# Starting every SBUF tile on a multiple of 128 bytes in a retention + GLU + SwiGLU kernel

## The chip, the cores and the metric

The kernel runs on one core of one Trainium2 chip. The metric is the time of one execution on the device in microseconds. Before the change three runs took 669.10, 670.97 and 668.92 us, median 669.1 us.

## The reference

Three stages follow one another. Retention: per batch and head a state is decayed by gamma and grows by the outer product of key and value; the output is the query times the state. Then a feed-forward layer, `(a * b) @ w_out`, on 1536 tokens of width 512 with hidden width 1536. Then RMS normalisation with a gain, and a second layer with a SiLU gate.

```python
for t in range(S):                       # S = 768, 2 batches, 8 heads, head_dim 64
    state = gamma * state + k[t] outer v[t]
    y[t] = q[t] @ state / sqrt(64)
x = y.reshape(1536, 512)
x = ((x @ w_a) * (x @ w_b)) @ w_out                       # first layer, d_ff 1536
xn = x / sqrt(mean(x * x) + 1e-6) * rms_g
out = (silu(xn @ w_gate) * (xn @ w_val)) @ w_out2         # second layer
```

## The kernel before

**Numbers.** Every operand of the two layers is held as a pair of fp32r tiles, `hi` and `lo`, whose sum is the value, and each product is made of three matmuls: hi*hi, hi*lo and lo*hi. `x_tiles` allocates the pairs of activations (`xh`, `xl`, in the second layer `nh`, `nl`), `conv_w` makes the pairs of weights (`wh`, `wl`), and `second` in `up` makes the pairs of hidden values (`hh`, `hl`).

**Units.** The work of the layers is cut into 72 units, in the order of layer, weight group `g` (4), token block `j` (3 blocks of 512 tokens) and hidden block `f` (3 of a group). A unit issues two runs of 12 matmuls in `up_half` (lines 170 to 172: four blocks of the width, three matmuls each), each with 512 columns, and later, in `down`, another 12 (lines 214 to 216 in the first layer, 218 to 220 in the second). So a unit has 36 matmuls of 512 columns and all units 72 x 36 = 2592. The `down` of a unit comes two or three units after its `up` (`LAG2`, `LAG`). In the up runs and the first layer's downs the weights are the stationary operand and the activations move; in the second layer's downs the hidden values are stationary and the weights move.

**Two sets of weight tiles.** A weight block `c` goes to `wps[c % RING]`, with `RING` 6: blocks 0 to 2 of each six, which are the groups with even `g`, go to the pool `wp`, which is made at the start; blocks 3 to 5, the groups with odd `g`, go to the pool `wq`, which is made after the retention (line 466). Half of the units, 36, work on `wp` tiles, and the other half on `wq` tiles. In time the groups alternate: even, odd, even, odd in either layer.

**Where the tiles lie.** The tiles of a pool lie end to end in a partition, in the order of first allocation, each begun on a multiple of 32 bytes; a pool that is closed (the retention's `ac`, `ap`, `a2`) gives its space to the pools made after it (`yp`, `wq`). The first tile, `rg_sb`, has 4 numbers (16 bytes) in each partition, and takes 32. `dk_sb` has 192 bytes and `gq_sb` 96. All other tiles that matter here have multiples of 512 bytes, but for the five small tiles of the normalisation (`me`, `t`, `r`, `rh`, `rl`, 16 bytes each, in `yp` ahead of `wq`). The program's list of allocations gives these byte addresses in the partition:

| tiles | first address | remainder by 128 | by 512 |
|---|---|---|---|
| `rg_sb` | 16512 | 0 | 128 |
| `ones`, `ones32`, `ident` | 16544 | 32 | 160 |
| `xh`, `xl`, `nh`, `nl` (pool `xp`) | 18080 | 32 | 160 |
| `wh`, `wl` in `wp` | 67232 | 32 | 160 |
| `hh`, `hl` and the other hidden tiles | 104096 | 32 | 160 |
| `raw`, `u`, `v`, `z` (pool `cp`) | 124576 | 32 | 160 |
| `dq_sb`, later `acc` of block 1 | 159392 | 32 | 160 |
| `dk_sb`, `gq_sb` | 161952, 162144 | 32, 96 | 160, 352 |
| `q`, `k`, `qd`, `vd`, `p`, `sd` of the retention | 162752 | 64 | 448 |
| `sq`, `d` | 175776 | 32 | 160 |
| `me`, `t`, `r`, `rh`, `rl` | 188064 | 32, 64, 96, 0, 32 | |
| `wh`, `wl` in `wq` | 188224 | 64 | 320 |

**Engines beside TensorE.** `conv_w` turns a loaded raw weight block (64-bit numbers) into a pair: two passes on ScalarE (lines 120, 121), five on VectorE (123 to 125, 134, 138), one on GpSimd (126), one more on ScalarE (136). 72 blocks are converted. `norm` squares a block's sums, adds them up by matmuls with `ones32` (264), computes the reciprocal root with a refinement step on tiles of 4 numbers (267 to 275), spreads it by a diagonal (278, GpSimd) and a matmul (284), and scales (290 to 294). The DMAs of the loads are issued by SyncE, those of the constants at the start by ScalarE. The order on each engine is that of the program text (`manual_schedule`).

Of the kernel before, what the change touches and what calls it, by code (L numbers as in the profile page):

```python
# [7 lines left out]
F32 = mybir.dt.float32  # L8
# [7 lines left out]
B, H, S, D = 2, 8, 768, 64  # L16
P = 128
# [5 lines left out]
CPB = S // C  # L23
NP = H // 2
KD = DM // P
NF = DFF // P
TB = 512
NB = NT // TB
CPT = TB // C
TPB = TB // P  # L30
# [9 lines left out]
BEGIN = {0: (1, 1), 1: (1, 1), 2: (0, 1)}  # L40
BEGIN |= {i: (i in (10, 13, 16, 19, 22), 1) for i in (*range(3, 34), *range(39, 66))}
LAG = 3
SIGN = -(1 << 31)

PARTS = KD, TPB
# [3 lines left out]
def retention_glu_swiglu(ctx: ExitStack, tc: tile.TileContext, qk, kv, dq, tri, dk, gq, eye, w1, w2, rg, out):  # L49
# [19 lines left out]
    cst = ctx.enter_context(tc.tile_pool(name="cst", bufs=1))  # L69
# [5 lines left out]

    y0 = ctx.enter_context(tc.tile_pool(name="y0", bufs=1))

    rg_sb = cst.tile([P, KD], F32, name="rg_sb")
    ones = cst.tile([P, P], F32R, name="ones")
    ones32 = cst.tile([P, P], F32, name="ones32")  # L80
    ident = cst.tile([P, 1, P], F32, name="ident")

    xs = {}

    def x_tiles(j, what):
        hi = xp.tile([P, KD, TB], F32R, tag="xh", name=f"{what}h{j}")
        lo = xp.tile([P, KD, TB], F32R, tag="xl", name=f"{what}l{j}")
        xs[what, j] = (hi, lo)
# [18 lines left out]
    def conv_w(i):  # L107
# [15 lines left out]
        nc.vector.tensor_scalar(ui, ui, 3, 0x7FFFFFFF, op0=ALU.logical_shift_left, op1=ALU.bitwise_and)  # L123
        nc.vector.scalar_tensor_tensor(ui, upper, SIGN, ui, op0=ALU.bitwise_and, op1=ALU.bitwise_or)
        nc.vector.tensor_scalar(zi, ui, -(1 << 23), None, op0=ALU.bitwise_and)  # L125
# [24 lines left out]
    def step(todo=beside):  # L150
        for g in list(todo):
            if next(g, g) is g:
                todo.remove(g)
# [21 lines left out]
    def up(i):  # L175
# [13 lines left out]
        def second():  # L189
            b = up_half(i, 1)  # L190
            h = hp.tile([P, TB], F32, tag="h", name=f"h{i}")
            hh = hp.tile([P, TB], F32R, tag="hh", bufs=LAG, name=f"hh{i}")
            hl = hp.tile([P, TB], F32R, tag="hl", bufs=LAG, name=f"hl{i}")
            nc.vector.tensor_tensor(h, b, gate[0], op=ALU.mult)  # L194
# [27 lines left out]
    def collect(i):  # L222
        ffn, g, j, f = units[i]
        if f % GRP < GRP - 1:
            return
        if g == 0:
            acc[ffn, j] = (yp if j else y0).tile([P, *((TPB, DM) if ffn else (KD, TB))], F32, tag=f"acc{j}", name=f"acc{ffn}_{j}")
        for m in range(PARTS[ffn]):
            collect_part(ffn, g, j, m)
        if ffn == 0 and g == NG - 1:  # L230
            norming.append(norm(j))
# [17 lines left out]
    def norm(j):  # L249
        y = acc[0, j]  # L250
        sq = yp.tile([P, KD, TB], F32, tag="sq", name=f"sq{j}")
        d = yp.tile([P, 2, TB], F32R, tag="d", name=f"d{j}")
        me, t, r, rh, rl = (yp.tile([P, TPB], F32, tag=w, name=f"{w}{j}") for w in ("me", "t", "r", "rh", "rl"))
        nc.scalar.activation(sq[:, 0:2, :], y[:, 0:2, :], AF.Square)
        nc.scalar.activation(sq[:, 2:4, :], y[:, 2:4, :], AF.Square)
        yield
        yield
        nc.vector.tensor_tensor(sq[:, 0:2, :], sq[:, 0:2, :], sq[:, 2:4, :], op=ALU.add)
        nc.vector.tensor_tensor(sq[:, 0, :], sq[:, 0, :], sq[:, 1, :], op=ALU.add)
        for _ in range(4):  # L260
            yield
        ms = sp.tile([P, TB], F32, tag="S", name=f"ms{j}")
        for c in range(TPB):
            nc.tensor.matmul(ms[:, c:c + 1], sq[:, 0, c * P:(c + 1) * P], ones32[:, 0:1], start=True, stop=True)
        yield

        nc.vector.tensor_scalar(me, ms[:, 0:TPB], 1.0 / DM, 1e-6, op0=ALU.mult, op1=ALU.add)
        nc.scalar.activation(t, me, AF.Sqrt)
        yield
        nc.vector.reciprocal(r, t)  # L270
        nc.vector.tensor_tensor(t, r, r, op=ALU.mult)
        nc.vector.scalar_tensor_tensor(t, t, -0.5, me, op0=ALU.mult, op1=ALU.mult)
        nc.vector.scalar_tensor_tensor(r, t, 1.5, r, op0=ALU.add, op1=ALU.mult)
        nc.vector.tensor_copy(rh.bitcast(F32R), r)
        nc.vector.tensor_tensor(rl, r, rh, op=ALU.subtract)

        for i, w in enumerate((rh, rl)):
            nc.gpsimd.tensor_tensor(d[:, i].rearrange("p (c t) -> p c t", t=P), ident.to_broadcast([P, TPB, P]), w[:, :, None].to_broadcast([P, TPB, P]), op=ALU.mult)
        yield
        yield  # L280
        yield
        rb = sp.tile([P, TB], F32, tag="S", name=f"rb{j}")
        for i in range(2):
            nc.tensor.matmul(rb, ones, d[:, i], start=(i == 0), stop=(i == 1))
        yield
        x_tiles(j, "n")
        hi, lo = xs["n", j]
        for e in range(0, KD, 2):
            for k in (e, e + 1):
                nc.vector.scalar_tensor_tensor(y[:, k, :], y[:, k, :], rg_sb[:, k:k + 1], rb, op0=ALU.mult, op1=ALU.mult)  # L290
            nc.scalar.copy(hi[:, e:e + 2, :], y[:, e:e + 2, :])
            yield
            for k in (e, e + 1):
                nc.gpsimd.tensor_tensor(lo[:, k, :], y[:, k, :], hi[:, k, :].bitcast(F32), op=ALU.subtract)
        normed.add(j)
# [3 lines left out]
    def unit(i):  # L299
# [3 lines left out]
        for n, f in enumerate(up(i)):  # L303
# [6 lines left out]
            if n == 0:  # L310
                due(i - (LAG if i < 4 * GRP else LAG2))
                step()

    def due(i):
        while nd[0] <= i:
            for m in range(PARTS[units[nd[0]][0]]):
                down(nd[0], m)
            collect(nd[0])
            nd[0] += 1

    with tc.manual_schedule():

        with ExitStack() as att:
            ac = att.enter_context(tc.tile_pool(name="ac", bufs=1))
# [3 lines left out]

            dq_sb = ac.tile([P, NP, C], F32, name="dq_sb")
            tri_sb = ac.tile([P, 1, C], F32, name="tri_sb")  # L330
            dk_sb = ac.tile([P, CPB, H], F32, name="dk_sb")
            gq_sb = ac.tile([P, CPB, NP], F32, name="gq_sb")
            st = sp.tile([P, B, NP, D], F32, name="st")
            qk_t, kv_t = {}, {}

# [76 lines left out]
            w = ps.tile([P, P], F32, tag="A", name="w")  # L412
# [52 lines left out]
        yp = ctx.enter_context(tc.tile_pool(name="yp", bufs=1))  # L465
# [59 lines left out]
```

## Time and profile before

| what | value |
|---|---|
| median of three runs | 669.1 us (668.92 to 670.97) |
| profiled execution, its own time | 669.5 us |
| its span, first to last instruction | 667.7 us |
| TensorE matmul busy | 653.4 us, 98% |
| VectorE busy | 427.1 us, 64% |
| ScalarE busy | 255.6 us, 38% |
| GpSimd busy | 166.3 us, 25% |
| mean granted TensorE clock | 0.992 |

Busy shares are averages over the span. A matmul's busy time in the profile runs to its modelled end, and the ends overlap the next start: a 512-column matmul is shown with some 390 ns, while one starts every 0.23 us. What a matmul costs is therefore read from the distance of starts, that is from the number of matmuls in a stretch or from the chain of work, and not from the mean duration. The chain of work gives starts in steps of 0.01 us, so a spacing is taken over a dozen starts or more.

### The profile page before, as it was taken

The page shows a single profiled execution, that of the slowest core. Times are in us where ns is not written, and L with a number is a line of the kernel's source. Part 1 is how long each engine was busy: PE and PEld are TensorE (multiplying, and loading weights), DVE is VectorE, ACT ScalarE, POOL GpSimd, SP SyncE. Part 2 cuts the span into 40 slices and gives each one's busy share as a digit, 9 for nine tenths or more (in the row PEclk, how much of TensorE's full clock was granted, in tenths as well). Part 3 has the DMA queues.
Part 4 walks back from the last instruction along what each step waited for, and adds up shares of the span by engine and source line. Part 5 has one row for each costly group of instructions (what it writes and reads, how often), then busy time and mean ns, then how long its engine had stood idle before and what let it go on. Part 6 is the DMA issues. An engine that isn't in the chain of part 4 may idle for free.

```text
span 667.7 us, 8594 instructions
## 1 busy us (share of the span) xinstructions
PE 653.4 (98%) x3342; PEld 533.3 (80%) x3342; DVE 427.1 (64%) x703; ACT 255.6 (38%) x436; POOL 166.3 (25%) x118
## 2 busy tenths in 40 slices
PE   7699999999999999999999999999999999999997
PEld 6588888888888888888887888888888888888885
DVE  4988545564876976665765657665665775775333
ACT  3555324444344443333443454443333333332110
POOL 3766211121221222211133225111111111111000
PEclk7899999999999999999999999999999999999999
DMA  9866121231332332222210012122122222200111
GB/s 353 299 234 242 36 64 64 63 96 31 95 95 64 95 95 68 67 61 61 65 60 0 1 31 64 63 64 64 63 64 63 64 63 64 64 31 1 63 64 63
DMA packets 16601, 54.47 MB, mean 82 GB/s; under 512 B 2224, under 2 KB 2736, under 8 KB 16560
## 3 DMA queue, kind: packets, MB, share of 16 engines
q1 hardware_dynamic: 15840, 53.42, 24.8%
q8 instruction: 26, 0.43, 0.3%
q10 hardware_dynamic: 720, 0.50, 0.2%
q14 instruction: 15, 0.12, 0.1%
HBM read 50.76 MB, written 3.15 MB: 81 GB/s over the span
## 4 chain that ended last, share of the span: by engine, by line
PE 91%; DVE 5%; DMA 2%; ACT 1%; POOL 1%; issue 1%; ACTq 0%; DVEq 0%; POOLq 0%
PE a L170 19%; PE a L171 19%; PE a L172 19%; PE y L218 5%; PE y L219 5%; PE y L220 5%; PE y L215 5%; PE y L214 5%; PE y L216 5%; PE ya L399 1%; DMA q<-in_qk 1%; PE ya L389 1%; DMA tri_sb<-in_tri 1%; PE sc L363 1%; DVE acc L241 1%; DVE p L365 1%
## 5 line engine op out<-in xcount | busy, mean ns | idle before, releaser
L126 POOL TENSOR_TENSOR v<-v,z 128x512 f32<-128x512 f32 x72 | 113.2, 1572 | 397.4 <-DVE z L125 397.4
L194 DVE TENSOR_TENSOR h<-a,g 128x512 f32<-128x512 f32 x72 | 49.8, 691 | 154.6 <-PE a L172 154.4
L171 PE MATMUL a<-xl,wh 128*128 128x512 f32 x288 | 113.5, 394 | 0.0
L170 PE MATMUL a<-xh,wh 128*128 128x512 f32 x288 | 113.3, 393 | 0.0
L171 PE MATMUL a<-nl,wh 128*128 128x512 f32 x288 | 113.2, 393 | 0.0
L170 PE MATMUL a<-nh,wh 128*128 128x512 f32 x288 | 113.0, 392 | 0.0
L172 PE MATMUL a<-nh,wl 128*128 128x512 f32 x288 | 112.9, 392 | 0.0
L172 PE MATMUL a<-xh,wl 128*128 128x512 f32 x288 | 112.6, 391 | 0.0
L136 ACT CAST wh<-u 128x512 fp32r<-128x512 f32 x72 | 44.7, 620 | 146.0 <-DVE u L134 145.8
L195 ACT CAST hh<-h 128x512 fp32r<-128x512 f32 x72 | 44.7, 620 | 124.4 <-DVE h L194 124.0
L134 DVE TENSOR_TENSOR u<-u,v 128x512 f32<-128x512 f32 x72 | 53.4, 741 | 28.6 <-POOL v L126 28.6
L170 PEld LDWEIGHTS a<-xh,wh 128*128 128x128 f32 x288 | 54.0, 188 | 13.0 <-issue 0.5
L170 PEld LDWEIGHTS a<-nh,wh 128*128 128x128 f32 x288 | 54.1, 188 | 12.4
L171 PEld LDWEIGHTS a<-nl,wh 128*128 128x128 f32 x288 | 54.1, 188 | 12.2
L172 PEld LDWEIGHTS a<-xh,wl 128*128 128x128 f32 x288 | 54.1, 188 | 12.2
L172 PEld LDWEIGHTS a<-nh,wl 128*128 128x128 f32 x288 | 54.1, 188 | 12.1
L171 PEld LDWEIGHTS a<-xl,wh 128*128 128x128 f32 x288 | 54.1, 188 | 11.8
L138 DVE TENSOR_TENSOR wl<-u,wh 128x512 fp32r<-128x512 f32 x72 | 58.6, 814 | 0.7 <-ACT wh L136 0.7
L215 PE MATMUL y<-hl,wh 128*128 128x512 f32 x144 | 56.8, 395 | 0.0
L197 DVE TENSOR_TENSOR hl<-h,hh 128x512 fp32r<-128x512 f32 x72 | 49.8, 692 | 10.9 <-ACT hh L195 10.7
L218 PE MATMUL y<-wh,hh 128*128 128x512 f32 x144 | 56.6, 393 | 0.0
L219 PE MATMUL y<-wl,hh 128*128 128x512 f32 x144 | 56.6, 393 | 0.0
(71 smaller groups left out, 916.4 us busy)
## 6 DMA issues: line engine op xcount, KB each, us to landing
raw<-in_w SPq DMA_DIRECT2D x72, 512.0 KB, 3.6
q<-in_qk SPq DMA_DIRECT2D x12, 512.0 KB, 5.9
k<-in_kv SPq DMA_DIRECT2D x12, 512.0 KB, 6.1
out<-acc SPq DMA_DIRECT2D x11, 256.0 KB, 2.2
dq_sb<-in_dq ACTq DMA_DIRECT2D x1, 256.0 KB, 4.0
out<-acc SPq DMA_DIRECT2D x1, 128.0 KB, 2.0
out<-acc ACTq DMA_DIRECT2D x1, 128.0 KB, 2.0
tri_sb<-in_tri ACTq DMA_DIRECT2D x1, 64.0 KB, 5.7
```

The source lines that it names most:

```text
L126: nc.gpsimd.tensor_tensor(v, v, z, op=ALU.mult)
L134: nc.vector.tensor_tensor(u, u, v, op=ALU.add)
L136: nc.scalar.copy(hi, u)
L138: nc.vector.tensor_tensor(lo, u, hi.bitcast(F32), op=ALU.subtract)
L170: nc.tensor.matmul(a, wh[:, c], xh[:, k, :], start=(k == 0), stop=False)
L171: nc.tensor.matmul(a, wh[:, c], xl[:, k, :], start=False, stop=False)
L172: nc.tensor.matmul(a, wl[:, c], xh[:, k, :], start=False, stop=(k == KD - 1))
L194: nc.vector.tensor_tensor(h, b, gate[0], op=ALU.mult)
L197: nc.vector.tensor_tensor(hl, h, hh.bitcast(F32), op=ALU.subtract)
L215: nc.tensor.matmul(y, dh[:, c], hl, start=False, stop=False)
L218: nc.tensor.matmul(y, hh[:, c], dh, start=s, stop=False)
L219: nc.tensor.matmul(y, hh[:, c], dl, start=False, stop=False)
```

## The change

`rg_sb` becomes a view of the first 4 numbers of a tile of 32 (128 bytes). The five small tiles of the normalisation become slices of one tile `small` of 64 numbers (256 bytes, 60 used: five kinds, three blocks, four numbers) in the constants' pool, with a place of its own for each block; before, a kind had one place that the three blocks used in turn. `dk_sb` and `gq_sb` become views of tiles of 256 and 128 bytes. No instruction is added or taken away, no shape, engine or order is changed.

By the sizes, every tile then begins on a multiple of 128 bytes. The tiles of the layers (`xh`, `xl`, `nh`, `nl`, both weight pools, `hh`, `hl`, `acc`, `sq`, `d`) come to a remainder of 0 by 512: `xp` begins at 16512 + 128 + 3 x 512 + 256 = 18432, `wq` at 188416. The retention's tiles come to a remainder of 0 by 128 and 384 by 512.

```diff
 LAG = 3
+
+LINE = 128
 SIGN = -(1 << 31)
@@
-    rg_sb = cst.tile([P, KD], F32, name="rg_sb")
+
+    rg_sb = cst.tile([P, LINE // 4], F32, name="rg_sb")[:, :KD]
     ones = cst.tile([P, P], F32R, name="ones")
     ones32 = cst.tile([P, P], F32, name="ones32")
     ident = cst.tile([P, 1, P], F32, name="ident")
+    small = cst.tile([P, 2 * LINE // 4], F32, name="small")[:, :5 * NB * TPB].rearrange("p (w j t) -> p w j t", j=NB, t=TPB)
@@
-        me, t, r, rh, rl = (yp.tile([P, TPB], F32, tag=w, name=f"{w}{j}") for w in ("me", "t", "r", "rh", "rl"))
+        me, t, r, rh, rl = (small[:, i, j, :] for i in range(5))
@@
-            dk_sb = ac.tile([P, CPB, H], F32, name="dk_sb")
-            gq_sb = ac.tile([P, CPB, NP], F32, name="gq_sb")
+            dk_sb = ac.tile([P, LINE // 2], F32, name="dk_sb")[:, :CPB * H].rearrange("p (c h) -> p c h", h=H)
+            gq_sb = ac.tile([P, LINE // 4], F32, name="gq_sb")[:, :CPB * NP].rearrange("p (c n) -> p c n", n=NP)
```

## Rows read from the trace of the kernel before

**Rows 1.** Page, busy time and share of each engine over the span.
```profile
PE 653.4 (98%) x3342; PEld 533.3 (80%) x3342; DVE 427.1 (64%) x703; ACT 255.6 (38%) x436; POOL 166.3 (25%) x118
```

**Rows 2.** Windows by stage: length, busy us (count) per engine, granted clock, DMA share, GB/s.
```profile
0.00:33.00 33.00, 23.12 (x273) 19.85 (x273) 21.81 (x31) 14.43 (x32) 18.29 (x19) 0.84 0.89 330
33.00:78.03 45.03, 44.86 (x522) 36.77 (x520) 38.84 (x59) 21.11 (x44) 25.24 (x18) 1.00 0.55 190
78.03:663.80 585.77, 585.42 (x2552) 476.66 (x2550) 365.64 (x612) 220.03 (x361) 122.81 (x81) 1.00 0.19 58
663.80:667.70 3.90, 0.00 (x0) 0.00 (x0) 0.77 (x3) 0.00 (x0) 0.00 (x0) 0.88 0.61 218
```

**Rows 3.** Windows of stretches on one set of weight tiles, TensorE's columns alone.
```profile
149.44:205.43 55.99, 55.99 (x241) 1.00 0.26 80
219.29:279.18 59.89, 59.89 (x266) 1.00 0.26 80
438.75:503.15 64.40, 64.40 (x277) 1.00 0.19 58
522.57:582.43 59.86, 59.86 (x265) 1.00 0.21 62
```

**Rows 4.** Chain of work, even group of the first layer: start, length, instruction.
```profile
103.94 0.23 PE a L172
104.17 0.23 PE a L170
...
106.66 0.23 PE y L216
106.89 0.23 PE y L214
```

**Rows 5.** Chain of work, odd group of the first layer.
```profile
159.87 0.23 PE y L216
160.10 0.23 PE y L214
160.33 0.24 PE y L215
...
162.90 0.23 PE a L170
```

**Rows 6.** Chain of work, last downs of the second layer, weights moving from wq.
```profile
658.18 0.23 PE y L218
...
661.45 0.25 PE y L220
```

**Rows 7.** Chain of work, return from a wq run to a wp run.
```profile
211.16 0.24 PE a L170
211.40 0.23 PE a L171
...
213.01 0.23 PE a L172
```

**Rows 8.** TensorE's waits: engine, line, releaser: us in total, times, longest.
```profile
PE ya L399 <- DVE p L365: 3.3, 2, 3.2
PE st L379 <- DVE vd L355: 2.3, 1, 2.3
PE sc L363 <- POOL qd L353: 1.7, 2, 1.1
PE ms L264 <- DVE sq L259: 0.3, 1, 0.3
```

**Rows 9.** Conversion's outputs to both sets of tiles: ns min/median/max, first and last start.
```profile
L136 ACT CAST wh<-u x72: 605/621/623, 17.8 to 613.1; 128x512 fp32r<-128x512 f32 x72
L138 DVE TENSOR_TENSOR wl<-u,wh x72: 675/682/1827, 21.0 to 616.8; 128x512 fp32r<-128x512 f32 x72
```

**Rows 10.** Normalisation's small tiles: ns min/median/max, first and last start us.
```profile
L267 DVE TENSOR_SCALAR me<-ms x3: 152/152/157, 333.1 to 387.9; 128x4 f32<-128x4 f32 x3
L278 POOL TENSOR_TENSOR d<-ident,rl x3: 1041/1042/1042, 337.7 to 391.0; 128x512 fp32r<-128x512 f32 x3
```

**Rows 11.** Chain of work, its DMA pieces in the opening; DMA issues with us to landing.
```profile
1.17 5.66 DMA tri_sb<-in_tri
6.84 6.28 DMA q<-in_qk
...
q<-in_qk SPq DMA_DIRECT2D x12, 512.0 KB, 5.9
k<-in_kv SPq DMA_DIRECT2D x12, 512.0 KB, 6.1
```

## The prediction

> **What bounds the kernel now.** I read the page's busy shares first, then windows by stage, then the spacing of matmuls within a stage, because the change touches addresses alone and can only act through how long an instruction takes. TensorE is busy for 98% of the span; the next engine, VectorE, for 64% [rows 1]. [...] Its named waits are 3.3 us or less each [rows 8], the first three in the retention, before 78 us. So from 78 us on the time is the number of matmuls times the distance of their starts, and nothing else is near: VectorE has 365.64 us of work in 585.77.
>
> **Does that distance depend on addresses?** The kernel before has a natural test, since the two sets of weight tiles lie at different remainders: `wp` at 32 by 128, as every other operand of the layers, and `wq` at 64. In a run on `wp` both operands of a matmul have the same remainder, in a run on `wq` they differ. Two stretches on `wp` alone (second and fourth of [rows 3]): 264 matmuls begin in each (22 runs of 12; the count shown holds one or two that were still running), so 59.89 / 264 = 226.9 ns and 59.86 / 264 = 226.7 ns. Two stretches on `wq` alone (first and third of [rows 3]): 55.99 / 240 = 233.3 ns and 64.40 / 276 = 233.3 ns. Same instruction, same shape, same clock. The chain shows it from start to start: 13 starts in 2.95 us, 226.9 ns [rows 4], against 13 in 3.03 us, 233.1 ns [rows 5]. It isn't the layer (each kind has a stretch in both), nor DMA load (0.26 in a fast stretch and in a slow one, 0.21 and 0.19 in the others). It isn't the side on which the tile is read either: in the last downs `wq` tiles move and the hidden values, at 32, are stationary, and 14 starts take 3.27 us, 233.6 ns [rows 6], like the up runs where `wq` is stationary. [...]
>
> **The change part by part.** *Addresses in the layers.* After it `wp`, `wq`, the activations and the hidden values all begin at 0 by 512, so that in every matmul the two operands agree, as they do now for `wp` (both at 160 by 512). That case I price by the rows of `wp`. Affected are the 36 units on `wq`, 36 x 36 = 1296 matmuls: 1296 x (233.3 - 226.7) = 1296 x 6.6 ns = 8.6 us, all of it on the path. The 1296 matmuls on `wp` keep their 226.7 ns.
>
> *Changeovers.* After a run on `wq` a run on `wp` isn't at 226.7 at once: eight starts take 1.85 us, 231.3 ns [rows 7], so a return costs 8 x 4.6 = 37 ns. At each of the seven borders between groups the downs lag two or three units behind, so that runs on both sets alternate, some 17 returns in all: 0.6 us. They go away. The same settling will be paid afresh where something breaks the stream within today's slow stretches (the normalisation's matmuls), some four times 37 ns, 0.15 us. Net 0.5 us.
>
> *Other engines.* Half of the 72 outputs of lines 136 and 138 go to tiles at 32, half to 64. Line 136 lies between 605 and 623 ns for all of them, and line 138 has a minimum of 675 and a median of 682 [rows 9]. So I take no effect on VectorE and ScalarE, from 32 to 0 as from 32 to 64. Bound: 18 ns, the spread of line 136, each way on 72 blocks' seven passes, 9 us of engine time, but hidden under TensorE, since VectorE and ScalarE have over 200 us to spare there; without that cover it would all count.
>
> *The shared tile `small`.* It adds no instruction. If the scheduler orders accesses by whole tile, a block's first write (line 267) waits for GpSimd's last read in the block before (line 278); three blocks lie between 333.1 and 387.9 us, with reads of 1.04 us right after [rows 10], so the previous read is long done. Within a block GpSimd's first read could wait for line 275, the next of six small VectorE instructions, under 0.2 us. Queued behind it is only GpSimd's own conversion work, and TensorE has its units meanwhile. Cost nought; without cover, at most 3 x 0.2 us.
>
> *The opening.* DMA landings stand on the path with 5.66 + 6.28 = 11.9 us [rows 11]. The retention's own operands keep their differences to one another, and the loads write to 0 instead of 64. No row shows a DMA at 0 against one at 64; the two equal loads of 512 KB land in 5.9 and 6.1 us, so I bound the effect by that 3%, 0.4 us either way, and take nought. `rg_sb`, `dk_sb` and `gq_sb` move the same bytes.
>
> *Sum.* 8.6 + 0.5 = 9.1 us. The profiled execution took 669.5 us, 1.8 around its span of 667.7, and would take 660.4. It lies 0.4 above the median of the runs, 669.1, from which the sum is 660.0. I give 660.2.
>
> What is late next is TensorE again: VectorE's 64% becomes 65%.
>
> **The rivals.** *A: the remainder isn't the cause, no change.* `wq` tiles also all lie above byte 188000 of the partition, all other operands of the layers below byte 125000. If the place in the memory and not the remainder sets the spacing, nothing moves: 669.1 us. [...]
>
> *B: slower, the remainder counts in itself.* Tiles at 64 would be slow because they begin on a whole 64 bytes, and 0 does that too. Then all 2592 matmuls take 233.3 ns or more, and the 1296 on `wp` lose what `wq` loses now: 669.1 + 8.6 = 677.7 us, and more if both operands' costs add up. The time changes by 2592 x (S - 230.0) ns, where S is the new spacing and 230.0 the mean of 226.7 and 233.3: it is slower from S = 230 ns on. Against it: 64 on either side costs the same, and 64 with 32 was never compared with 64 with 64 in a settled stretch, so it isn't excluded.
>
> *C: faster than forecast.* At 0 the remaining overhead shrinks as well. No row has a pair at 0; a step of the same 6.6 ns on all 2592 is 17.1 us more, 643 us. That the spacing holds at 226.7 in all settled stretches of both layers speaks for a floor.
>
> [...]
>
> **How the numbers follow.** Forecast 0.68, A 0.13, B 0.11, C 0.08. Around the forecast: 0.4 us for the opening each way, 0.5 for the settling, 0.4 for the two bases, and gains kept by parts of the runs only, so 657.5 to 663 holds it. With A, up to 669.8 (the median and its nearer spread), the range holds 0.81: 657.5 to 669.8. About 0.3%, 2 us, is what a measurement of this kernel can tell from no change. Faster by more than that: forecast and C, 0.76; within: A, 0.13; slower: B, 0.11.
>
> **What would show it.** In the stretches on `wq` the spacing is 226.7 ns instead of 233.3 and the chain shows every third piece no longer at 0.24; the stretches on `wp` stay as they are; lines 136 and 138 keep 621 and 682 ns; the time before 78 us stays within half a microsecond. Wrong, and by A, if odd groups stay at 233.3; by B, if the even groups go up to that; by C, if the even groups fall below 226.

## The result and the profile after

The changed kernel took 658.95 us (median of four runs, 658.27 to 661.01) against 669.01 us beside it: a ratio of 0.985, 95% interval 0.982 to 0.988. Two later sets of runs gave 0.9855 (0.9836 to 0.9874) and 0.9846 (0.9831 to 0.9860). It is faster by 10 us; 8.9 us were forecast.

The span fell from 667.7 to 656.8 us. The page of the changed kernel, busy time of each engine as in [rows 1]:

```profile
PE 644.5 (98%) x3342; PEld 534.1 (81%) x3342; DVE 425.3 (65%) x703; ACT 255.5 (39%) x436; POOL 165.6 (25%) x118
```

The counts are the same, TensorE lost 8.9 us of busy time, and no other engine moved by more than 2 us. By stage, in windows cut at the same matmuls as in [rows 2] (length, busy us and count per engine, granted clock, DMA share, GB/s):

```profile
0.00:33.00 33.00, 24.50 (x272) 20.99 (x272) 22.64 (x33) 14.57 (x32) 18.13 (x19) 0.95 0.87 330
33.00:77.16 44.16, 44.16 (x523) 36.51 (x521) 38.70 (x57) 20.95 (x43) 24.82 (x18) 1.00 0.56 194
77.16:653.00 575.84, 575.82 (x2552) 476.59 (x2550) 363.22 (x612) 219.96 (x361) 122.67 (x81) 1.00 0.20 59
653.00:656.80 3.80, 0.00 (x0) 0.00 (x0) 0.78 (x3) 0.00 (x0) 0.00 (x0) 1.00 0.61 228
```

The reader sees where the 10.9 us of span went: 585.77 - 575.84 = 9.9 us in the layers, with the same 2552 matmuls, 78.03 - 77.16 = 0.9 us before them, 0.1 us behind them. The four stretches of [rows 3], cut at the same matmuls (240, 264, 276 and 264 begin in them; the count shown holds one or two more that were still running):

```profile
148.01:202.41 54.40, 54.40 (x242) 1.00 0.28 83
216.01:275.85 59.84, 59.84 (x266) 1.00 0.27 80
432.50:495.06 62.56, 62.56 (x277) 1.00 0.20 60
514.10:573.94 59.84, 59.84 (x265) 1.00 0.21 62
```

All four are at 226.7 ns now (54.40 / 240, 59.84 / 264, 62.56 / 276, 59.84 / 264). The first and third, on `wq`, were at 233.3; the other two were there already. The chain of work in an odd group, where [rows 5] showed 0.24 at every third piece (lines are four higher in the changed file, so L174 is the old L170):

```profile
159.05 0.23 PE a L174
159.28 0.23 PE a L175
159.50 0.23 PE a L176
...
161.09 0.23 PE a L174
```

Nine starts take 2.04 us, 226.7 ns. Lines 140 and 142 write the weight pairs, which [rows 9] showed as lines 136 and 138 (ns min/median/max):

```profile
L140 ACT CAST wh<-u x72: 604/621/625, 18.9 to 603.9; 128x512 fp32r<-128x512 f32 x72
L142 DVE TENSOR_TENSOR wl<-u,wh x72: 677/682/1818, 21.1 to 607.4; 128x512 fp32r<-128x512 f32 x72
```

The medians are unchanged: for these two passes of ScalarE and VectorE the addresses did nothing.

### The profile page after: what moved, and what is told of

Same layout as the page of the kernel before. It is cut to its first block, busy times and chain, and to the rows that moved or that the text cites. A ratio compares the mean times of both kernels' runs of the same rounds, so it can differ in the third digit from the quotient of the medians.

```text
span 656.8 us, 8593 instructions
## 1 busy us (share of the span) xinstructions
PE 644.5 (98%) x3342; PEld 534.1 (81%) x3342; DVE 425.3 (65%) x703; ACT 255.5 (39%) x436; POOL 165.6 (25%) x118
## 4 chain that ended last, share of the span: by engine, by line
PE 95%; DVE 2%; DMA 2%; issue 1%; POOL 0%; ACTq 0%; DVEq 0%; POOLq 0%
PE a L174 20%; PE a L175 20%; PE a L176 20%; PE y L220 5%; PE y L219 5%; PE y L218 5%; PE y L223 5%; PE y L224 5%; PE y L222 5%; PE sc L367 1%; PE ya L403 1%; PE ya L393 1%; DMA q<-in_qk 1%; DMA tri_sb<-in_tri 1%; PE st L383 1%
## 5 line engine op out<-in xcount | busy, mean ns | idle before, releaser
L174 PE MATMUL a<-xh,wh 128*128 128x512 f32 x288 | 112.7, 391 | 0.0
L174 PE MATMUL a<-nh,wh 128*128 128x512 f32 x288 | 112.3, 390 | 0.0
L175 PE MATMUL a<-xl,wh 128*128 128x512 f32 x288 | 112.1, 389 | 0.0
L176 PE MATMUL a<-nh,wl 128*128 128x512 f32 x288 | 112.1, 389 | 0.0
L176 PE MATMUL a<-xh,wl 128*128 128x512 f32 x288 | 112.1, 389 | 0.0
L174 PEld LDWEIGHTS a<-xh,wh 128*128 128x128 f32 x288 | 54.1, 188 | 11.8 <-issue 0.5
L174 PEld LDWEIGHTS a<-nh,wh 128*128 128x128 f32 x288 | 54.1, 188 | 11.3
L176 PEld LDWEIGHTS a<-nh,wl 128*128 128x128 f32 x288 | 54.1, 188 | 11.2
L176 PEld LDWEIGHTS a<-xh,wl 128*128 128x128 f32 x288 | 54.1, 188 | 11.2
L201 DVE TENSOR_TENSOR hl<-h,hh 128x512 fp32r<-128x512 f32 x72 | 49.9, 692 | 10.9 <-ACT hh L199 10.8
L218 PE MATMUL y<-hh,wh 128*128 128x512 f32 x144 | 56.0, 389 | 0.0
```

The source lines that it names most:

```text
L174: nc.tensor.matmul(a, wh[:, c], xh[:, k, :], start=(k == 0), stop=False)
L175: nc.tensor.matmul(a, wh[:, c], xl[:, k, :], start=False, stop=False)
L176: nc.tensor.matmul(a, wl[:, c], xh[:, k, :], start=False, stop=(k == KD - 1))
L201: nc.vector.tensor_tensor(hl, h, hh.bitcast(F32), op=ALU.subtract)
L218: nc.tensor.matmul(y, dh[:, c], hh, start=s, stop=False)
```

## The experiments

All of them compute the reference in full; they change addresses alone, but for the last one, which moves a step.

**Only `wq` moved.** The kernel before with an unused tile in front of `wq`; nothing lies at 0 that did not before, and the layers' tiles are all at 32 by 128.

```diff
+        gap = ctx.enter_context(tc.tile_pool(name="gap", bufs=1))
+        gap.tile([P, 24], F32, name="gap")
         wps += [ctx.enter_context(tc.tile_pool(name="wq", bufs=1))] * (RING - GRP)
```

> The kernel before with one unused gap of 96 bytes in front of wq and nothing else: wq lies at 32 by 128 as the other operands of the layers, no tile of the layers lies at 0, the retention's tiles and the small tiles stay where they were. Theory (difference of the two addresses): odd groups at 226.7 ns, the time of the changed kernel, 659 to 660.5 us. Rival A (the place in the memory): odd groups stay at 233.3 ns, 669 us. Rival (only a start on whole lines of 128 bytes helps): 669 us too.

659.29 us, ratio 0.9852 (0.9836 to 0.9867). An odd and an even stretch, cut as above:

```profile
148.74:203.14 54.40, 54.40 (x242) 1.00 0.27 84
216.74:276.58 59.84, 59.84 (x266) 1.00 0.28 81
```

The gap alone gives the whole gain: rival A falls, since the tiles are still at the high end of the memory, and so does any reading in which tiles must start on whole lines. By 512 the gap brings `wq` to 188320, a remainder of 416, while the other operands are at 160: the two are 256 apart, so over whole stretches 256, at 54.40 / 240 = 226.7 ns, is as good as 0. The changed kernel, run beside it:

> The changed kernel again, beside the others on one chip. Theory (the spacing of matmuls depends on the difference between the addresses of the moving and the stationary operand by 128): some 10 us under the kernel before, ratio 0.985, every stretch of the layers at 226.7 ns. Left open by the first run is where about 1 us of the gain before 78 us comes from: if from the addresses of the retention's tiles, the kernel with only wq moved (e2_wq_only) must stay 1 us above this one; if from the way the opening happens to fall, the two are alike.

659.31 us (658.97 to 662.25). The two are alike, so the other three edits of the change, which move the small tiles and the retention's, bring nothing that can be measured.

**All tiles at 64.** `rg_sb` padded to 64 bytes instead of 128:

```diff
-    rg_sb = cst.tile([P, LINE // 4], F32, name="rg_sb")[:, :KD]
+    rg_sb = cst.tile([P, LINE // 8], F32, name="rg_sb")[:, :KD]
```

> The changed kernel with the first tile padded to 64 bytes instead of 128: every tile of the layers and of the retention begins at 64 by 128, none at 0. Theory (difference): 226.7 ns everywhere, the time of the changed kernel, 659 to 660 us. Rival B (64 is slow in itself, and the remainder counts for each operand): 233.3 ns or more on all 2592 matmuls, 675 us or more.

660.93 us (658.83 to 662.31), ratio 0.9867 (0.9849 to 0.9885). Its stretches:

```profile
148.89:203.29 54.40, 54.40 (x242) 1.00 0.27 84
216.89:276.73 59.84, 59.84 (x266) 1.00 0.27 81
```

226.7 ns in both, with every operand at 64: rival B falls. The 1.6 us by which its median lies over the changed kernel's isn't spacing; what its trace shows of it is told below.

**One set off by 32.** The changed kernel with a gap of 32 bytes (`gap.tile([P, 8], ...)`) in front of `wq`:

> The changed kernel with an unused gap of 32 bytes in front of wq: wq at 32 by 128, all else at 0. Theory (difference): odd groups back at about 233 ns, 667.5 to 669 us, though most tiles begin on whole lines; even groups stay at 226.7 ns. Rival (whole lines of the moving operand or of most tiles are what counts): 659 to 664 us.

668.22 us, ratio 0.9984 (0.9975 to 0.9993). The stretches:

```profile
149.41:205.41 56.00, 56.00 (x242) 1.00 0.27 81
219.18:279.03 59.85, 59.85 (x265) 1.00 0.26 81
```

56.00 / 240 = 233.3 ns on `wq`, 226.7 on `wp`, as before the change. So the difference between the addresses of the two operands sets the spacing, not the address of either.

**Which differences.** Gaps between the tiles of `wq`, of 32, 64, 96 and 128 bytes in all ahead of its first, second and third block's up tiles and its down tiles:

```diff
+    gaps = {(3, 0): 8, (4, 0): 8, (5, 0): 8, (3, 2): 8}
@@
+        if (c % RING, s) in gaps:
+            wp.tile([P, gaps.pop((c % RING, s))], F32, tag=f"gap{c % RING}_{s}", name=f"gap{i}")
         hi = wp.tile([P, DM], F32R, tag=f"h{c % RING}_{s}", name=f"wh{i}")
```

> The changed kernel with unused gaps between the tiles of wq, so that its tiles lie at several differences to the activations (by 512): the up tiles of its first, second and third weight block at 32, 64 and 96, the down tiles at 128. Theory (difference by 128): up runs at about 233 ns with the first and the third block, whose difference is 32 and 96; the downs, at 128, at 226.7 ns. The second block, at 64, tells whether a line of 64 bytes would do: 226.7 ns if it does, 233 ns or another value if 128 is needed. Time between 660 and 666 us.

668.53 us beside 668.00 of the kernel before, one run each, and above the 660 to 666 expected. Windows of twelve matmuls each, at 32, 64, 96 and 128 in this order (the count holds one or two more):

```profile
126.01:128.80 2.79, 2.79 (x13) 1.00 0.00 0
134.33:137.13 2.80, 2.80 (x14) 1.00 0.00 0
142.67:145.47 2.80, 2.80 (x13) 1.00 0.44 165
206.82:209.61 2.79, 2.79 (x13) 1.00 0.56 138
```

2.79 to 2.80 us for twelve is 232.5 to 233.3 ns at all four, 128 too. That was expected otherwise, and it is against the name of the change: a whole line of 128 bytes is no better than 32. The second map, at 256, 288 and 16 (up tiles) and 64 (down tiles):

```diff
+    gaps = {(3, 0): 64, (4, 0): 8, (5, 0): 56, (3, 2): 16}
@@
+        w = DM + 128 if (c % RING, s) in ((5, 0), (5, 1)) else DM
+        o = 4 if w > DM else 0
-        hi = wp.tile([P, DM], F32R, tag=f"h{c % RING}_{s}", name=f"wh{i}")
+        hi = wp.tile([P, w], F32R, tag=f"h{c % RING}_{s}", name=f"wh{i}")[:, o:o + DM]
```

(`lo` likewise, and the lines on `gaps` as above.)

> The changed kernel with other differences in wq: up tiles of its first block at 256, of the second at 288 (32 by 128), of the third at 16, the down tiles at 64. Theory (difference by 128): first block at 226.7 ns, second at about 233 ns as with 32; the third, at 16, above 226.7 ns if any step off a whole line costs, and at 226.7 ns if only whole 32 bytes count. Time between 660 and 666 us.

666.46 us beside 668.00, one run each. Windows of twelve at 256, 288, 16 and 16 again; then the last 23 starts of the last downs, where `wq` tiles at 64 move past stationary tiles at 0:

```profile
151.55:154.27 2.72, 2.72 (x13) 1.00 0.00 0
134.98:137.78 2.80, 2.80 (x14) 1.00 0.00 0
171.01:173.81 2.80, 2.80 (x14) 1.00 0.60 158
148.83:151.55 2.72, 2.72 (x13) 1.00 0.33 136
655.19:660.47 5.28, 5.28 (x24) 1.00 0.01 4
```

256 is as good as 0: 2.72 / 12 = 226.7 ns. 288 is like 32. At 16 one run of twelve goes at 233.3 ns and another at 226.7, and the tile of the quick run is back at 2.80 us for twelve from 176.60 on; what decides was not followed. With `wq` moving, 5.28 / 23 = 229.6 ns, so the two signs of 64 aren't alike here.

**Whole lines, but 128 apart.** The changed kernel with a gap of 128 bytes (`gap.tile([P, 32], ...)`) in front of `wq`:

> The changed kernel with an unused gap of 128 bytes in front of wq: every tile still begins on a whole line of 128 bytes, but wq lies 128 off the activations by 512 (and by 256). The theory of the prediction, a difference by 128: odd groups at 226.7 ns, the time of the changed kernel, 659 us. The theory after the map of differences, where 256 was as good as 0 and the downs at 128 were not: odd groups at 232 to 233 ns, 1296 x 5.7 to 6.6 ns = 7.4 to 8.6 us more, 666.5 to 668.5 us; then it isn't the whole lines that the change lives on.

668.89 us beside 669.55, ratio 0.9991 (0.9981 to 1.0000). Its stretches:

```profile
149.36:205.14 55.78, 55.78 (x241) 1.00 0.27 81
218.99:278.86 59.87, 59.87 (x265) 1.00 0.28 81
```

55.78 / 240 = 232.4 ns on `wq`. Every tile begins on a whole line of 128 bytes and nothing is gained. The change works because its paddings bring all the layers' tiles to the same remainder by 256; the lines themselves are beside the point.

**The lo weights alone off by 32.** The changed kernel with wider tiles for the `lo` half of `wq`'s up weights, used from byte 32 on:

```diff
+        w = DM + 128 if c % RING >= GRP and s < 2 else DM
+        o = 8 if w > DM else 0
-        lo = wp.tile([P, DM], F32R, tag=f"l{c % RING}_{s}", name=f"wl{i}")
+        lo = wp.tile([P, w], F32R, tag=f"l{c % RING}_{s}", name=f"wl{i}")[:, o:o + DM]
```

> The changed kernel with the lo tiles of the up weights in wq begun 32 bytes later, the hi tiles where they are. In a run of three (hi*hi, hi*lo, lo*hi) one matmul in three has a lo tile as its weights. If the weights that are being loaded for the next matmul get in the way of the columns now moving, the interval of the second matmul (line 175), during which the lo tile is loaded, is the long one; if it is a matmul's own weights, the interval of the third (line 176). By the theory about 7 to 16 ns in one of three intervals of the up runs in odd groups (864 matmuls): 2 to 3 us over the changed kernel, 661 to 662.5 us.

664.89 us in its one run, 5.9 us over the changed kernel's 658.95, about twice what was expected; the kernel before, run once beside it, took 668.00. The chain (L176 to L178 are the old lines 170 to 172):

```profile
150.02 0.23 PE a L176
150.26 0.24 PE a L177
150.50 0.23 PE a L178
150.72 0.23 PE a L176
150.96 0.24 PE a L177
...
153.52 0.23 PE a L176
```

The longest piece is L177's, while the shifted lo tile is loaded for the matmul after it (in the timeline of the kernel before, line 172's load begins at 133.64 us, 0.01 after line 171's matmul), as the first reading of the expectation has it. But that doesn't show the reading, since in the kernel before, where all three weight tiles are off, the piece in the middle is the long one too:

```profile
133.56 0.23 PE a L170
133.80 0.24 PE a L171
134.03 0.23 PE a L172
```

And five runs of three take 3.50 us, 233.3 ns on average: one tile of three off costs as much as all three off (864 x 6.6 ns = 5.7 us, near the 5.9 measured). So the cost isn't a price for each bad pair; all that the runs show is that the whole stream is slower. What slows it stays open. The records speak only against a load that itself lasts longer. Line 171 of the kernel before, in the first stretch of [rows 3] (on `wq`) and in the second (on `wp`):

```profile
L171 PEld LDWEIGHTS a<-xl,wh x52: 187/188/188, 149.4 to 204.7; 128*128 128x128 f32 x52
L171 PE MATMUL a<-xl,wh x52: 399/399/399, 149.7 to 205.0; 128*128 128x512 f32 x52
L171 PEld LDWEIGHTS a<-xl,wh x61: 187/188/188, 219.3 to 279.2; 128*128 128x128 f32 x61
L171 PE MATMUL a<-xl,wh x60: 389/389/397, 219.5 to 278.7; 128*128 128x512 f32 x60
```

The load takes 188 ns on either set; the matmul's record grows, from 389 to 399 ns.

**The scatter of the changed kernel.** Its runs lie between 658.3 and 662.3 us. In the trace of the run beside the experiments TensorE waits at line 268 for VectorE's sum of squares, in the first trace it doesn't. First the first trace, then the other (start, length, instruction, idle before):

```profile
375.84 3.08 POOL L298 TENSOR_TENSOR nl<-acc,nh 128x512 fp32r<-128x512 f32 x2 [3.04 <-ACT nh L295]
375.84 0.69 DVE L263 TENSOR_TENSOR sq<-sq 128x512 f32<-128x512 f32 x1
...
376.58 1.05 PE L268 MATMUL ms<-ones,sq 128*128 128x1 f32 x8
```

```profile
375.91 2.96 POOL L298 TENSOR_TENSOR nl<-acc,nh 128x512 fp32r<-128x512 f32 x2 [3.03 <-ACT nh L295]
375.92 1.82 DVE L263 TENSOR_TENSOR sq<-sq 128x512 f32<-128x512 f32 x1
...
377.79 1.05 PE L268 MATMUL ms<-ones,sq 128*128 128x1 f32 x8 [0.99 <-DVE sq L263]
```

VectorE and GpSimd begin within 0.01 us of each other in both. Where GpSimd's record begins clearly ahead, VectorE's 0.69 us become 1.82, and TensorE waits 0.99 us. The twelve traces have 24 such pairs, and in the records' nanoseconds they part cleanly: in nine GpSimd begins 6 to 13 ns ahead, and VectorE takes 1.82 to 1.83 us; in 15 it begins 2 to 5 ns ahead, or 2 ns behind, and VectorE takes 0.69 us. The turn thus lies at a lead of between 5 and 6 ns. What makes it turn there is not shown. The race is not new with the change: the kernel before lost 0.3 us to it in its trace [rows 8], and the kernel with `wq` 128 apart, which gained nothing, lost more:

```profile
PE ms L268 <- DVE sq L263: 1.2, 2, 0.9
```

In the kernel with all tiles at 64 the same wait was followed by a fall of the granted clock (TensorE's windows):

```profile
376.00:379.90 3.90, 2.91 (x18) 1.00 0.00 0
379.90:383.30 3.40, 3.40 (x10) 0.52 0.00 0
```

Eight matmuls there take 427 ns each instead of 227, 1.6 us in all, at a granted clock of 0.52, after TensorE had stood for 1.0 of 3.9 us. This trace is of the slowest of that kernel's four runs, 662.31 us, and its stretch from 78 us on also begins at 78.04 us, 0.9 later than in the changed kernel's first trace. Wait, clock and late opening make up 3.5 of the 3.7 us between the two spans (660.5 and 656.8); that the runs without a trace scatter for the same reasons is not shown. The attempt to take the wait away, by one step more before line 268 for the last block, which moves all that follows in that block's normalisation by a step:

```diff
-        for _ in range(4):
+        for _ in range(5 if j == NB - 1 else 4):
             yield
```

> The changed kernel with one step more between the squares' sum on VectorE and the matmuls of line 268, for the last token block alone (line 264: five steps instead of four): TensorE does 12 matmuls of a unit before it comes to the wait. Theory (the scatter of the changed kernel, 658.3 to 662.3, is VectorE's sum at line 263 taking 1.8 instead of 0.7 us in some executions, so that TensorE waits 1.0 us at line 268, now and then with a fall of the granted clock behind it): no wait there in the trace, the slow end of the runs goes, median 0.3 to 0.8 us under the changed kernel. Rival (the wait turns up elsewhere in the normalisation, or the scatter comes from the opening): median the same within 0.3 us.

662.56 us (661.98 to 662.85), beside it the changed kernel:

> The changed kernel once more, to set beside the two others of this call: 658.3 to 662.3 us, median about 659.2.

659.07 us (658.74 to 659.78). So it is 3.5 us slower. TensorE's waits that are new in it:

```profile
PE a L175 <- POOL nl L298: 1.2, 2, 0.7
PE rb L288 <- POOL d L282: 0.9, 2, 0.5
```

The wait at line 268 isn't there, but VectorE's sum was quick in this trace, so that it would have been missing without the step too:

```profile
L263 DVE TENSOR_TENSOR sq<-sq x3: 692/692/693, 322.6 to 375.8; 128x512 f32<-128x512 f32 x3
```

The theory of the scatter is thus not tested by it. What it shows is that the block's normalised values now come after TensorE wants them: 2.1 of the 3.5 us are the new waits above. Of the rival, that the wait turns up elsewhere in the normalisation held, and that the time stays the same did not. The step of 12 matmuls cost more than the wait it was to remove.

## Why the prediction was right, and where it was not

*What bounds.* TensorE's distance of starts times the number of matmuls: right, the gain is in the layers with the same count, 2552, and the same granted clock, 1.00.

*The price of an address.* 6.6 ns for 1296 matmuls, 8.6 us: the two `wq` stretches lost 1.59 us on 240 and 1.84 us on 276, 6.6 and 6.7 ns. The step that carried the sum held.

*Changeovers.* 0.5 us net were put down. Added up from start to start over the two traces, the 9.9 us of the layers are 8.7 on the matmuls of odd groups, 0.7 on those of even groups, where the returns to `wp` lie, and 0.5 around the normalisation's matmuls, 0.3 of it the wait of [rows 8] that the first trace of the changed kernel doesn't have. The sum had 8.6 and 0.5 for the first two, 9.1 against 9.4 measured, so the term was of the right kind and some 0.3 us too small. The 0.5 of the normalisation was not in the sum, and its wait is the race told above: luck of the two executions, and not the change.

*The opening.* Nought was forecast, within 0.4 us, and the layers' long stretch began 0.87 us earlier: this is the term that was missed. The addresses of the retention's tiles alone don't decide it. In the kernels with a gap of 32 and of 128 in front of `wq`, whose retention tiles lie exactly as in the changed kernel, that stretch begins at 78.13 and 78.05 us, like the 78.03 before; in the changed kernel's three traces it begins at 77.16, 77.22 and 77.27, and in the map with 32, 64 and 96 at 77.14. With `wq` alone moved it begins at 77.89, and the time was that of the changed kernel all the same, so the 10 us don't hang on the opening. Nor does the granted clock of the first 33 us decide, 0.95 in the changed kernel's first trace and 0.84 in its last. The stretch begins either near 77.2 or near 78.0 us; what does decide was not found.

*Other engines, the shared tile.* Nothing, as said: the medians of lines 140 and 142 stand at 621 and 682 ns, and moving `wq` alone gives the same time.

*Where the reason was too wide.* The sum priced a pair of operands that agree by 512, which is what the change makes, and that was safe. That a change made for multiples of 128 ends at 0 by 512 is luck of the tiles' sizes. But the text also spoke of remainders by 128, and that is not the rule: 128 apart costs 5.7 ns (232.4 against 226.7), and only 0 and 256 were quick in every settled stretch. A reader who had taken the whole line of 128 bytes for the cause would have forecast 659 us for the kernel with the gap of 128, as the first theory in that run's expectation does; it took 668.9. The runs show that the difference of the two addresses sets the spacing, 226.7 ns at 0 and 256 and 232.4 to 233.3 ns on `wq` 32, 128 and 160 apart; by what in the chip is not shown.

*Rivals.* A and B are excluded by the kernel with `wq` alone moved and the one with all tiles at 64, both at 226.7 ns. C, a further step, did not come: 226.7 ns is the lowest settled spacing in every kernel run here. That addresses matter is measured with nothing else changed: the kernel with `wq` off by 32 differs from the changed kernel only in where one operand lies, and the starts on `wq` are 233.3 ns apart instead of 226.7.

*What is late next.* "TensorE again" was right, with an addition that the forecast lacked: a race of some nanoseconds between VectorE and GpSimd in the normalisation costs TensorE 0.3 to 1.0 us, before the change as after it.

## What to carry to other kernels

Where TensorE runs without a gap, compare the distance of starts between stretches of the same shape: if two sets of tiles differ, look at where the moving and the stationary operand of a matmul lie to each other, and bring them to the same remainder by 256 bytes (here 226.7 ns at differences of 0 and 256, 232.4 at 128), which one small tile or gap in front of a pool can do (here 96 bytes in front of `wq`, 659.29 us against 669.34). A small tile of 16 or 96 bytes ahead of the large ones shifts everything after it, as `rg_sb` and `gq_sb` do here, and a test that shifts one pool alone, once by a good and once by a bad amount, shows in two runs whether it matters.

## What the runs showed of the hardware that was not expected

- The spacing of this kernel's 512-column fp32r matmuls, each with a weight load of its own, depends on the difference between the two operands' byte addresses: 226.7 ns at 0 and 256, 232.4 to 233.3 ns with stationary weights 32, 64, 96, 128, 160 (the kernel before) and 288 ahead, both values at 16, and 229.6 ns with moving weights 64 ahead. The load itself is 188 ns at 0 and at 160.
- One weight load in three from a tile at a difference of 32 slowed the whole stream to the same 233.3 ns average as three in three.
- Where VectorE's sum of squares (128x512) starts beside GpSimd's `nl`, it took 1.82 to 1.83 us in the nine pairs in which GpSimd's record leads by 6 to 13 ns, and 0.69 us in the 15 with a lead of 5 ns or less, in twelve traces.
- After a wait of 1.0 us TensorE's granted clock fell to 0.52 for a window of 3.4 us in one execution (all tiles at 64, mean clock 0.989), and not in another with the same wait (the changed kernel beside it, mean clock 0.997).
